# Repacking 64-bit tables in 26 pieces of 512 columns, with the low halves subtracted on VectorE and the raw weight loads behind the gathers

## The chip, the cores and the metric

One core of one Trainium2 chip runs the whole program. The metric is the device time of one execution in microseconds (us). Engines are named as in the profile: PE is TensorE's matrix multiply, PEld its weight load, DVE is VectorE, ACT is ScalarE, POOL is GpSimd, SP is SyncE, which here only issues DMAs.

## The reference

Three layers follow one another, on 2 batches of 768 tokens with 512 channels.

- Attention with 8 heads of 64: each token sees a local window of 96 tokens and 8 global ones, with a bias that falls with distance; then a softmax and the product with v.
- A mixture of 8 experts (512 to 1024 to 512, relu): each token goes to the expert with the largest logit, or to the one of the token before it, as a gate says; the result is weighted by the softmax of the logits.
- A mixing layer. With `theta = x @ w_theta` it is

```
zr, zi = x * cos(theta), x * sin(theta)
y = w_tok_r @ zr + w_tok_i @ zi          # over the 768 tokens of a batch
u = x + y
out = u + relu(u @ w_ch)
```

The three tables of the last layer, `w_theta` (512 x 512), `w_tok` (1536 x 768, r and i stacked) and `w_ch` (512 x 512), reach the chip as 64-bit floats. The kernel makes of each number a 32-bit float, and splits that into a high part (fp32r) and a low part, since its matmuls run in fp32r, three of them for one product.

## The kernel before, in words

**Attention** (lines 431 to 964). 24 steps of two units each; a unit is two heads of one block of 128 tokens. In a step PE makes the scores (`qk`, L542), DVE adds the bias and takes the maximum (`soft`, L564), ACT takes the exponential (L574), PE transposes (L597) and multiplies with v (L621). The routing of earlier blocks is put between (`route_stages`). A list, TAIL, orders what is left after step 23, with the work of a first group of 128 tokens ("lead") on PE. SP issues the loads of q, k, v.

**Experts** (lines 966 to 1601). The experts are taken by their number of tokens, ranks r = 0 to 7. Rows of x are gathered from DRAM by POOL's indirect DMA (`gather_x`, L1004) and transposed by PE (`x_tr`, L1288). The loop `for u in range(64)` takes a slice of 128 hidden units of rank r = u // 8: `mm1(u + 2)` (L1443, or L1427 for the small ranks), `mm2(u)` (L1480, L1490), `split_w1(u + 3)`, `split_w2(u + 1)`, `relu(u + 2)` (L1457, L1462). In ranks 0 to 3 w1 is split in two as well (ACT L1313, DVE L1314); w2 is split in all ranks (ACT L1410, then L1411 on POOL for ranks 0 to 3 but for u = 1, and on DVE for ranks 4 to 7). The raw weights come in 32 pieces of two 512 KB loads each, issued by SP in the order of the program (`load_piece`, L988 for w1, L992 for w2), with three buffers of each kind. SP reads the expert's number from `order_i` into a register before a load (L981). At u = 1 SP stores the weights of the tokens (`pd`, L1580); POOL gathers them back by slot (`gather_p`, L1354).

**Table jobs** (lines 354 to 418). A job repacks 256 columns of 128 rows: a load into `jraw`, ACT L391 (absolute value), DVE L392, L394, L396, L398 (put the 32 bits together, drop what is too small), ACT L401 (high part), and POOL L404 (low part). There are 52 jobs, w_theta first, then w_tok by rows, then w_ch. A job is a generator: `job_tick` runs it up to its next `yield`, so its steps are spread by hand over the program. After L401 a job issues the load of the job two further on. In the expert loop each u has 6 ticks and a job takes 10 of them (JLAG); in the last layer there are 18 places (JT), and `job_upto` forces what is due.

**Mixing layer** (lines 1604 to 1926). Twelve blocks k of 128 tokens. In the turn of block k PE does `h_mix(k, 0..3)` (48 matmuls of L1736), `h_theta(k + 2)` (L1660) and a transposition; DVE, ACT and POOL make sine and cosine of block k + 2 (`trig_*`, L1670 to L1716, of which L1692 and one L1716 are on POOL). `h_u` adds the sums of a batch, `h_out` makes the output (L1773).

Of the kernel before, what the change touches and what calls it, by code (L numbers as in the profile page):

```python
# [95 lines left out]
def kernel(  # L96
# [257 lines left out]
    jobs = []  # L354

    def add_jobs(src, dst, c, width):
        for o in range(0, width, 256):
            jobs.append((src[c * 128 : (c + 1) * 128, o : o + 256], dst, c, o))

    for c in range(4):  # L360
        add_jobs(w_theta, wth, c, DM)
    for t in range(NT):
        for c in (t, NT + t):
            add_jobs(w_tokT, None, c, S)
    for c in range(4):
        add_jobs(w_ch, wch, c, DM)

    def job_to(k):
        _, dst, c, o = jobs[k]
        return [(dst[i][:, c] if dst else wtok(i, c))[:, o : o + 256] for i in range(2)]  # L370
# [12 lines left out]
    def job(k):

        t = jraw.pop(k)
        lo, hi = t[:, :, 0], t[:, :, 1]
        w = jpool[0].tile([128, 256], I32, tag="jw", name="jw", bufs=2)
        m = jpool[0].tile([128, 256], F32, tag="jm", name="jm", bufs=2)
        wf = w.bitcast(F32)
        wh, wl = job_to(k)  # L390
        A.activation(m, hi.bitcast(F32), AF.Abs)  # L391
        V.tensor_scalar(w, hi, 3, 0x3FFFFFFF, op0=ALU.logical_shift_left, op1=ALU.bitwise_and)  # L392
        yield
        V.scalar_tensor_tensor(w, lo, 29, w, op0=ALU.logical_shift_right, op1=ALU.bitwise_or)  # L394
# [1209 lines left out]
    with ExitStack() as hctx:  # L1604
# [187 lines left out]
        ticks = {"n": 0, "done": 0, "per": nj / JT}

        def tick(n):
            ticks["n"] += n * ticks["per"]
            while ticks["done"] < ticks["n"]:
                job_tick()
                ticks["done"] += 1
# [192 lines left out]
```

## Time and profile before

| | |
|---|---|
| three runs | 525.34, 518.68, 524.3 us; median 524.3 us |
| the profiled execution | 524.86 us in all |
| its span, first to last instruction | 522.7 us |
| busy | PE 490.7, DVE 377.8, ACT 268.5, POOL 194.4 us |
| stages, us from the span's start | attention to 125, expert ranks 0 to 3 to 247, ranks 4 to 7 to 330, mixing layer to 522.7 |

The span leaves 2.2 us of the execution's own time around it. Busy time is an average over stages with different limits. A busy PE need not be a PE at its peak: the profile gives the clock that it was granted in a separate column (PEclk; 1.00 is 2.4 GHz, 0.50 is 1.2 GHz).

### The profile page before, as it was taken

What the parts mean: (1) busy time and instruction counts of PE and PEld (TensorE: products, weight loads), DVE (VectorE), ACT (ScalarE), POOL (GpSimd) and SP (SyncE); (2) the same over time, 40 slices, a digit from 0 to 9 for tenths busy, and PEclk for the clock granted to TensorE, in tenths of its full rate; (3) what the DMA queues carried; (4) which work ended last, traced back from release to release, by engine and by line L of the source; (5) the groups of instructions that cost most, each with busy time, mean ns of one, the idle gap of its engine ahead of it and who ended that gap; (6) DMA issues with size and microseconds to landing.
All of it is one profiled execution on the core that took longest, in us unless ns stands there. A gap on an engine that the chain in (4) does not pass through costs nothing.

```text
span 522.7 us, 9734 instructions
## 1 busy us (share of the span) xinstructions
PE 490.7 (94%) x3328; PEld 392.3 (75%) x3330; DVE 377.8 (72%) x1005; ACT 268.5 (51%) x686; POOL 194.4 (37%) x224
## 2 busy tenths in 40 slices
PE   9999999997979899899999999999998899999994
PEld 4676767686767788788777776788877688888884
DVE  6778787673957999789675868557888997672421
ACT  5886867513535756475545566445455444640200
POOL 3002223121656858476432325203444434360400
PEclk9999999998997999799999999999999989999999
DMA  8776759128557877666888986320122210001122
GB/s 242 244 204 205 234 183 324 46 73 276 145 131 250 271 222 252 216 227 198 283 278 270 289 281 226 97 81 20 25 76 82 80 42 20 22 0 50 33 95 72
DMA packets 65226, 83.20 MB, mean 159 GB/s; under 512 B 6816, under 2 KB 41248, under 8 KB 65168
## 3 DMA queue, kind: packets, MB, share of 16 engines
q1 hardware_dynamic: 54244, 61.18, 37.3%
q10 hardware_dynamic: 8156, 14.29, 8.3%
q0 software_dynamic: 2768, 7.02, 4.7%
q8 instruction: 28, 0.46, 0.4%
q14 instruction: 30, 0.25, 0.2%
HBM read 71.14 MB, written 11.34 MB: 158 GB/s over the span
## 4 chain that ended last, share of the span: by engine, by line
PE 55%; DVE 24%; DMA 7%; ACT 7%; issue 5%; ACTq 0%; POOL 0%; DVEq 0%
PE a L1736 10%; PE b L1773 6%; PE h L1427 6%; PE o L1480 6%; PE h L1443 4%; PE x L621 3%; DVE jw L396 3%; DVE jw L394 3%; PE s L542 3%; PE pt L597 3%; PE o L1490 3%; DMA jraw<-in_w_theta_dram 3%; DMA jraw<-in_w_tokT_dram 2%; DVE w1s L1314 2%; PE th L1660 2%
## 5 line engine op out<-in xcount | busy, mean ns | idle before, releaser
L1736 PE MATMUL a<-wtokr,z 128*128 128x512 f32 x480 | 86.1, 337 | 0.1
L1736 PEld LDWEIGHTS a<-wtokr,z 128*128 128x128 f32 x480 | 73.4, 188 | 10.0 <-POOL wtokr L404 0.4
L1480 PE MATMUL o<-w2s,hh 128*128 128x512 f32 x192 | 66.6, 426 | 3.3 <-POOL w2s L1411 2.9
L1443 PE MATMUL h<-xT,w1s 128*128 128x256 f32 (+1 forms) x384 | 60.0, 306 | 8.1 <-DVE w1s L1314 7.5
L1443 PEld LDWEIGHTS h<-xT,w1s 128*128 128x128 f32 x384 | 54.1, 204 | 13.4 <-DVE w1s L1314 10.2
L574 ACT ACTIVATE pr<-sm,st 128x256 f32<-128x256 f32 (+1 forms) x96 | 46.0, 481 | 19.2 <-DVE st L564 18.2
L1411 POOL TENSOR_TENSOR w2s<-raw,w2s 128x512 fp32r<-128x512 f32 x31 | 42.6, 1376 | 28.6 <-ACT w2s L1410 26.8
L404 POOL TENSOR_TENSOR wtokr<-jw,wtokr 128x256 fp32r<-128x256 f32 x30 | 24.1, 803 | 61.7 <-ACT wtokr L401 61.7
L1427 PE MATMUL h<-xT,raw 128*128 128x192 f32 (+1 forms) x256 | 46.0, 323 | 0.0
L564 DVE CUSTOM_DVE_ANT_0 sm<-s,bias 128x256 f32<-128x256 f32 (+1 forms) x96 | 34.0, 396 | 13.7 <-PE s L542 13.5
L1427 PEld LDWEIGHTS h<-xT,raw 128*128 128x128 f32 x256 | 38.5, 190 | 7.0 <-issue 6.6
L1410 ACT ACTIVATE w2s<-raw 128x512 fp32r<-128x512 f32 x64 | 39.7, 621 | 3.0 <-ACT yo L1526 2.7
L1480 PEld LDWEIGHTS o<-w2s,hh 128*128 128x128 f32 x192 | 34.0, 194 | 8.2 <-POOL w2s L1411 3.7
L394 DVE SCALAR_TENSOR_TENSOR jw<-jraw,jw 128x256 int32<-128x256 int32 x52 | 37.8, 727 | 1.6
L1480 PE MATMUL o<-w2s,hl 128*128 128x512 f32 x96 | 38.8, 405 | 0.0
L1457 ACT ACTIVATE hh<-h 128x256 fp32r<-128x256 f32 (+1 forms) x64 | 20.8, 324 | 30.9 <-PE h L1443 17.1
L396 DVE SCALAR_TENSOR_TENSOR jw<-jraw,jw 128x256 int32<-128x256 int32 x52 | 34.7, 667 | 0.9
L392 DVE TENSOR_SCALAR jw<-jraw 128x256 int32<-128x256 int32 x52 | 25.0, 480 | 12.5 <-DMA jraw<-in_w_theta_dram 6.8
L1314 DVE TENSOR_TENSOR w1s<-raw,w1s 128x512 fp32r<-128x512 f32 x32 | 29.6, 925 | 3.6 <-ACT w1s L1313 2.9
L391 ACT ACTIVATE jm<-jraw 128x256 f32<-128x256 f32 x52 | 22.2, 427 | 17.4 <-DMA jraw<-in_w_tokT_dram 8.9
L1411 DVE TENSOR_TENSOR w2s<-raw,w2s 128x512 fp32r<-128x512 f32 x33 | 23.2, 704 | 10.2 <-ACT w2s L1410 9.7
L398 DVE SCALAR_TENSOR_TENSOR jw<-jm,jw 128x256 f32<-128x256 f32 x52 | 26.7, 514 | 3.4 <-DVE jw L396 0.5
(266 smaller groups left out, 997.3 us busy)
## 6 DMA issues: line engine op xcount, KB each, us to landing
raw<-in_w_dram SPq DMA_DIRECT2D x64, 512.0 KB
jraw<-in_w_tokT_dram ACTq DMA_DIRECT2D x33, 256.0 KB
vv<-in_pack_dram SPq DMA_DIRECT2D x10, 512.0 KB
w<-in_w_dram SPq DMA_DIRECT2D x16, 256.0 KB
kall<-in_pack_dram SPq DMA_DIRECT2D x10, 320.0 KB
xd<-xt SPq DMA_DIRECT2D x12, 256.0 KB
q<-in_pack_dram SPq DMA_DIRECT2D x11, 256.0 KB
yd<-yo ACTq DMA_DIRECT2D x11, 256.0 KB
```

What stands on the lines that cost most here:

```text
L394: V.scalar_tensor_tensor(w, lo, 29, w, op0=ALU.logical_shift_right, op1=ALU.bitwise_or)
L396: V.scalar_tensor_tensor(w, hi, -1073741824, w, op0=ALU.bitwise_and, op1=ALU.bitwise_or)
L564: V.tensor_tensor_reduce(out=sm[:, hh, 0:W], in0=ust[u]["s"][hh], in1=bias[:, 2 * j + hh], scale=-0.125, scalar=BIG, op0=ALU.add, op1=ALU.min,
L574: A.activation(pr[:, hh, 0:W], sm[:, hh, 0:W], AF.Exp, bias=st[:, hh : hh + 1], scale=-1.0, accum_out=sums[n][:, 2 * j + hh : 2 * j + hh + 1],
L1314: (second or V).tensor_tensor(l1, s1, f32(h1), op=ALU.subtract)
L1410: A.activation(h2, bb[:, o], AF.Copy)
L1411: (V if RCAP[u // 8] <= FEW or u in W2V else G).tensor_tensor(l2, bb[:, o], f32(h2), op=ALU.subtract)
L1427: PE.matmul(hp[:, :N], lhsT=pieces[u // 2][1][:, j, o * 128 : (o + 1) * 128], rhs=x[:, j, :N], start=(j == 0), stop=(j == 3),)
L1443: PE.matmul(hp[:, :N], lhsT=wa[:, j], rhs=xa[:, j, :N], start=(k == 0), stop=(k == 11))
L1480: PE.matmul(out[:M], lhsT=ha[:, lo : lo + M], rhs=wa, start=(f == 0 and q == 0), stop=(f == 7 and q == 2),)
L1736: PE.matmul(acc[b][d][o], lhsT=za[:, d * 128 : (d + 1) * 128], rhs=wa[:, lo:hi], start=(t == 0 and n == 0 and (o == 0 or d % 2 == 0)), sto ...
L1773: PE.matmul(op[:, : hi - lo], lhsT=wa[:, d, e * 128 : (e + 1) * 128], rhs=ua[d][:, lo:hi], start=(n == 0), stop=(n == 11),)
```

## The change

- The tables are cut in 26 jobs of 512 columns; two ends of 256 columns of w_tok make one job with two loads. The first three jobs (the rows of w_tok for block 0) now run within attention, with their loads on SP's queue and the low part on POOL: one tick at the end of 15 of the steps, the rest ahead of TAIL.
- In the expert loop the ticks are metered: none in rank 0, 1.3 a slice in ranks 1 to 3, 2.4 in ranks 4 to 7 (up to u = 60). A job now takes 6 ticks. In the mixing layer there are 6 ticks a block.
- All low parts of w2, and from the experts on those of the jobs, are subtracted on DVE.
- The second raw load (w2 of piece 0) moves into the list LOADS, behind the first three gathers, and SP takes the experts' numbers from a copy that POOL makes after issuing those gathers.
- `pex` and `psum_` share memory with two tiles that are done.

```diff
-JT = 18
-JLAG = 5
-T0, T1, T2, T3 = 0, 2, 2, 14
+JATT = (4, 5, 6, 8, 9, 10, 12, 13, 14, 16, 17, 18, 20, 21, 22)
+JRATE = (0, 1.3, 1.3, 1.3, 2.4, 2.4, 2.4, 2.4)
+T1, T2, T3 = 2, 2, 2
...
-LOADS = ((1, 1), (1, 2), (2, 1), (2, 2))
+LOADS = ((1, 1), (0, 2), (1, 2), (2, 1), (2, 2))
...
+    def tok_ends(t):
+        def dst():
+            return [(wtokr[i][:, 2 * t - 2 : 2 * t] if t else wtok0[i])[:, :, 512:S] for i in range(2)]
+        return [w_tokT[c * 128 : (c + 1) * 128, 512:S] for c in (t, NT + t)], dst
+    tok_jobs = [[tok_piece(t, 0), tok_piece(t, 1), tok_ends(t)] for t in range(NT)]
+    jobs = tok_jobs[0] + [piece(w_theta, wth, c) for c in range(4)]
+    for t in range(1, NT):
+        jobs += tok_jobs[t]
+    jobs += [piece(w_ch, wch, c) for c in range(4)]
-    jstate = {"k": 0, "loaded": 0, "gen": None, "lag": JLAG, "bufs": 2, "eng": A}
+    jstate = {"k": 0, "loaded": 0, "gen": None, "bufs": 2, "eng": SP, "sub": G}
...
-            t = jpool[0].tile([128, 256, 2], I32, tag="jraw", name="jraw", bufs=jstate["bufs"])
+            t = jpool[0].tile([128, 512, 2], I32, tag="jraw", name="jraw", bufs=jstate["bufs"])
...
-        w = jpool[0].tile([128, 256], I32, tag="jw", name="jw", bufs=2)
-        m = jpool[0].tile([128, 256], F32, tag="jm", name="jm", bufs=2)
+        w = jtmp.tile([128, 512], I32, tag="jw", name="jw", bufs=1)
+        m = jtmp.tile([128, 512], F32, tag="jm", name="jm", bufs=1)
...
-        for _ in range(jstate["lag"]):
-            yield
+        yield
...
-        G.tensor_tensor(wl, wf, f32(wh), op=ALU.subtract)
+        jstate["sub"].tensor_tensor(wl, wf, f32(wh), op=ALU.subtract)
...
-            if s in (15, 16):
+            if s in (1, 2):
                 job_load()
+            if s in JATT:
+                job_tick()
...
+        job_upto(3)
...
-            regs[k] = SP.value_load(order_i[0:1, r : r + 1] if n else first_i, min_val=0, max_val=E - 1)
+            regs[k] = SP.value_load(order_g[0:1, r : r + 1] if n else first_i, min_val=0, max_val=E - 1)
...
-    load_piece(0)
+    load_piece(0, (1,))
     for n in range(1, 4):
         gather_x(n)
+    order_g = ct([1, 8], I32, "order_g")
+    G.tensor_copy(order_g, order_i)
...
-            (V if RCAP[u // 8] <= FEW or u in W2V else G).tensor_tensor(l2, bb[:, o], f32(h2), op=ALU.subtract)
+            V.tensor_tensor(l2, bb[:, o], f32(h2), op=ALU.subtract)
...
-        jstate["lag"] = JLAG
-        quick = [0]
+        jstate["eng"], jstate["sub"] = A, V
+        quick = [0.0]
...
-                if go:
-                    quick[0] += TF[min(r, 2) if r < 5 else 3]
+                if u < JL:
+                    quick[0] += JRATE[r] / 6
                     job_tick(int(quick[0]))
...
-                job_upto(8 + 6 * (k + 1))
+                job_upto(7 + 3 * k)
```

## Rows read from the trace of the kernel before

**Rows 1.** The page: PE's and the others' busy time; the chain by engine.
```profile
PE 490.7 (94%) x3328; PEld 392.3 (75%) x3330; DVE 377.8 (72%) x1005; ACT 268.5 (51%) x686; POOL 194.4 (37%) x224
...
PE 55%; DVE 24%; DMA 7%; ACT 7%; issue 5%; ACTq 0%; POOL 0%; DVEq 0%
```

**Rows 2.** Windows by stage: length, busy PE, PEld, DVE, ACT, POOL, clock, DMA share, GB/s.
```profile
18.30:91.30 73.00, 70.80 (x739) 51.54 (x736) 57.30 (x282) 57.25 (x189) 14.46 (x24) 1.00 0.74 225
...
125.00:164.70 39.70, 36.69 (x240) 29.57 (x240) 28.56 (x60) 16.66 (x39) 21.18 (x20) 0.87 0.63 177
164.70:247.50 82.80, 75.11 (x452) 65.56 (x449) 74.75 (x115) 51.26 (x114) 56.69 (x50) 0.96 0.72 230
247.50:330.00 82.50, 82.27 (x555) 59.00 (x555) 58.74 (x175) 44.98 (x111) 28.54 (x32) 1.00 0.80 261
...
353.40:388.10 34.70, 34.70 (x194) 29.94 (x193) 29.53 (x52) 18.14 (x38) 14.87 (x13) 1.00 0.12 33
388.10:431.30 43.20, 37.86 (x194) 31.15 (x193) 39.04 (x69) 20.30 (x44) 18.63 (x19) 0.96 0.24 73
```

**Rows 3.** Windows of tile jw alone: busy DVE, ACT, POOL, clock, DMA, GB/s.
```profile
125.00:164.70 39.70, 12.76 (x16) 1.64 (x4) 2.77 (x4) 0.87 0.63 177
164.70:247.50 82.80, 44.25 (x60) 6.22 (x15) 12.79 (x15) 0.96 0.72 230
247.50:330.00 82.50, 27.56 (x68) 7.01 (x17) 14.36 (x18) 1.00 0.80 261
353.40:445.00 91.60, 39.16 (x64) 6.67 (x16) 12.34 (x16) 0.98 0.17 49
```

**Rows 4.** Lines 394 and 392 by themselves: shortest, median and longest, ns.
```profile
L394 DVE SCALAR_TENSOR_TENSOR jw<-jraw,jw x52: 418/426/2852, 132.0 to 439.6; 128x256 int32<-128x256 int32 x52
...
L392 DVE TENSOR_SCALAR jw<-jraw x52: 277/291/1466, 131.0 to 438.1; 128x256 int32<-128x256 int32 x52
```

**Rows 5.** The timeline around 208 us: DVE and POOL.
```profile
207.44 2.18 DVE L396 SCALAR_TENSOR_TENSOR jw<-jraw,jw 128x256 int32<-128x256 int32 x1
...
208.05 1.27 POOL L1411 TENSOR_TENSOR w2s<-raw,w2s 128x512 fp32r<-128x512 f32 x1
```

**Rows 6.** The page's costliest groups: w2's low part on each of its engines.
```profile
L1411 POOL TENSOR_TENSOR w2s<-raw,w2s 128x512 fp32r<-128x512 f32 x31 | 42.6, 1376 | 28.6 <-ACT w2s L1410 26.8
...
L1411 DVE TENSOR_TENSOR w2s<-raw,w2s 128x512 fp32r<-128x512 f32 x33 | 23.2, 704 | 10.2 <-ACT w2s L1410 9.7
```

**Rows 7.** Groups by shape: w1's low part (164.7 to 247.5 us); L1676 at 512 columns.
```profile
L1314 DVE TENSOR_TENSOR w1s<-raw,w1s 128x512 fp32r<-128x512 f32 x22 | 22.3, 1014 | 2.7 <-ACT w1s L1313 2.3
...
L1676 DVE SCALAR_TENSOR_TENSOR rr<-kk,rr 128x512 f32<-128x512 f32 x10 | 6.9, 692 | 0.3
```

**Rows 8.** Waits of the whole span: us in total, times, longest.
```profile
DVE sm L564 <- PE s L542: 13.5, 16, 1.5
...
PE h L1443 <- DVE w1s L1314: 7.5, 7, 2.8
...
DVE jw L392 <- DMA jraw<-in_w_tokT_dram: 5.0, 5, 2.0
...
PE tr L1288 <- DMA xg<-xd,xidx: 2.9, 2, 1.8
```

**Rows 9.** The timeline from 153 to 159 us: POOL and DVE behind DMAs.
```profile
153.11 0.96 POOL L1354 DMA_INDIRECT ps<-pd,xidx  x1 [4.76 <-DMA pd<-ptok]
...
158.65 0.29 DVE L392 TENSOR_SCALAR jw<-jraw 128x256 int32<-128x256 int32 x1 [6.83 <-DMA jraw<-in_w_theta_dram]
```

**Rows 10.** Windows of one matmul line alone, L1443 and then L1736: busy PE, PEld.
```profile
222.55:227.95 5.40, 3.03 (x24) 2.96 (x24) 1.00 0.58 183
...
353.45:388.10 34.65, 25.66 (x146) 21.92 (x145) 1.00 0.12 32
388.20:431.20 43.00, 27.46 (x145) 22.34 (x144) 0.96 0.24 73
```

**Rows 11.** The chain of waits: a 256 KB load of jraw, issue to landing.
```profile
303.73 6.73 DMA jraw<-in_w_tokT_dram
```

More of the change, by code (lines that the diff above doesn't have):

```diff
@@ L47 @@
 TWO_PI = 6.283185307179586
-NJ1 = 52
 NWARM = 14
@@ L71 @@
 JL = 61
-TF = (1, 1, 1, 1)
 W0, W1 = 8, 0
-LOADS = ((1, 1), (1, 2), (2, 1), (2, 2))
+LOADS = ((1, 1), (0, 2), (1, 2), (2, 1), (2, 2))
 PU = 1
@@ L78 @@
 GP = 4
-W2V = (1,)
 HU = 36
-JF = 0
 XL = 0
@@ L352, in wtok, with piece, tok_piece @@
         return wtokr[i][:, 2 * t - 2 + n] if t else wtok0[i][:, n]
[L354 to L370, printed above, removed]
-    jstate = {"k": 0, "loaded": 0, "gen": None, "lag": JLAG, "bufs": 2, "eng": A}
+    def piece(src, dst, c):
+        return [src[c * 128 : (c + 1) * 128, 0:512]], lambda: [x[:, c] for x in dst]
+    def tok_piece(t, n):
+        c = n * NT + t
+        return [w_tokT[c * 128 : (c + 1) * 128, 0:512]], lambda: [wtok(i, c)[:, 0:512] for i in range(2)]
+    def tok_ends(t):
[8 more added lines that the diff above has]
+    jstate = {"k": 0, "loaded": 0, "gen": None, "bufs": 2, "eng": SP, "sub": G}
     jraw = {}
@@ L377, in job_load @@
         if k < len(jobs):
-            t = jpool[0].tile([128, 256, 2], I32, tag="jraw", name="jraw", bufs=jstate["bufs"])
-            jstate["eng"].dma_start(t, jobs[k][0].bitcast(I32).rearrange("p (c w) -> p c w", w=2))
+            t = jpool[0].tile([128, 512, 2], I32, tag="jraw", name="jraw", bufs=jstate["bufs"])
+            W = 512 // len(jobs[k][0])
+            for i, src in enumerate(jobs[k][0]):
+                jstate["eng"].dma_start(
+                    t[:, i * W : i * W + W], src.bitcast(I32).rearrange("p (c w) -> p c w", w=2)
+                )
             jraw[k] = t
@@ L386, in job @@
         lo, hi = t[:, :, 0], t[:, :, 1]
-        w = jpool[0].tile([128, 256], I32, tag="jw", name="jw", bufs=2)
-        m = jpool[0].tile([128, 256], F32, tag="jm", name="jm", bufs=2)
+        w = jtmp.tile([128, 512], I32, tag="jw", name="jw", bufs=1)
+        m = jtmp.tile([128, 512], F32, tag="jm", name="jm", bufs=1)
         wf = w.bitcast(F32)
-        wh, wl = job_to(k)
+        wh, wl = jobs[k][1]()
         A.activation(m, hi.bitcast(F32), AF.Abs)
@@ L398, in job @@
         V.scalar_tensor_tensor(wf, m, MIN64, wf, op0=ALU.is_ge, op1=ALU.mult)
-        for _ in range(jstate["lag"]):
-            yield
+        yield
+        wf = wf.rearrange("p (i c) -> p i c", c=wh.shape[-1]) if len(wh.shape) == 3 else wf
         A.activation(wh, wf, AF.Copy)
@@ L427 @@
     jctx = ExitStack()
-    jpool = [jctx.enter_context(tc.tile_pool(name="jb", bufs=1, reuse_waits="tile"))]
+    jtmp = jctx.enter_context(tc.tile_pool(name="jb", bufs=1, reuse_waits="tile"))
+    jpool = [jtmp]
     with ExitStack() as actx:
@@ L1018 @@
     slot0 = ct([128, 1], F32, "slot0")
-    pex = ct([128, NB, 8], F32, "pex")
-    psum_ = ct([128, NB], F32, "psum_")
+    pex = posall
+    psum_ = mxall
     def probs():
@@ L1550 @@
         relu(1)
-        jstate["lag"] = JLAG
-        quick = [0]
+        jstate["eng"], jstate["sub"] = A, V
+        quick = [0.0]
         for u in range(64):
             r, f = divmod(u, 8)
-            go = jstate["k"] * 64 <= u * NJ1 and JF <= u < JL
             def tick():
-                if go:
-                    quick[0] += TF[min(r, 2) if r < 5 else 3]
+                if u < JL:
+                    quick[0] += JRATE[r] / 6
                     job_tick(int(quick[0]))
@@ L1787 @@
         us[1] = [[wtok(i, c) for c in (0, NT, 1, NT + 1)] for i in range(2)]
-        nj = len(jobs) - jstate["k"]
-        jstate["lag"] = 1
         jstate["bufs"] = JBUFS
         jpool[0] = jctx.enter_context(tc.tile_pool(name="jb2", bufs=1, reuse_waits="tile"))
[L1792 to L1798, printed above, removed]
         for k in range(1, 4):
@@ L1897 @@
                 h_u(b, 1)
-            trig_a(k + 2, tick=lambda: tick(T0))
+            trig_a(k + 2)
             h_xh(k + 3)
@@ L1901 @@
             h_xl(k + 3)
-            tick(T1)
+            job_tick(T1)
             if k == HS:
@@ L1909 @@
             trig_b(k + 2)
-            tick(T2)
+            job_tick(T2)
             h_mix(k, 3)
@@ L1914 @@
             trig_c(k + 2)
-            tick(T3)
+            job_tick(T3)
             if k == HS:
```

## The prediction

> **What bounds the kernel now.** I read the page first, for who is busy: PE 490.7 of 522.7 us, and DVE next with 377.8; the chain that ended last lies 55% on PE and 24% on DVE [rows 1]. So PE sets the time and DVE interrupts it somewhere. The windows by stage say where [rows 2]. Attention (18.3 to 91.3) has PE at 70.8 of 73.0 us. Ranks 4 to 7 (247.5 to 330) have it at 82.27 of 82.5, at the full clock. The loss is in three other stretches: rank 0 (125 to 164.7) with 3.0 us of idle PE and a granted clock of 0.87; ranks 1 to 3 (164.7 to 247.5) with 7.7 us idle, a clock of 0.96 and DVE busy 74.75 of 82.8; and blocks k = 4 to 6 of the mixing layer (388.1 to 431.3) with 5.3 us idle, a clock of 0.96 and DVE 39.04 of 43.2.
>
> What DVE spends its time on there is read from tile jw alone [rows 3]. A job has four DVE instructions. Unhindered they take 0.291 + 3 x 0.426 = 1.57 us, by the medians [rows 4]. In ranks 4 to 7 they do: 27.56 us for 17 jobs, 1.62 each. In ranks 1 to 3 a job costs 44.25 / 15 = 2.95 us, in the mixing layer 39.16 / 16 = 2.45. The longest L394 took 2.85 us [rows 4]. The difference between the stages is POOL: where jobs are slow, POOL does 512-wide subtractions beside them. The timeline shows a case, a 0.42 us DVE step that lasts 2.18 us while a subtraction of 1.27 us runs on POOL [rows 5]. L1314 suffers as well: 1.014 us on average in ranks 1 to 3 [rows 7] against 0.704 for the same shape where POOL has no w2 work [rows 6], and PE waits 7.5 us for it [rows 8].
>
> The Trainium skill has a rule for it ("SBUF — State Buffer", section "Who interferes with whom"): a VectorE instruction with two SBUF inputs, or in a two-port mode, and a GpSimd instruction that reads SBUF shut each other out for their whole length, whichever began first. The trace agrees in kind (2.18 us above). By that rule all of the stretch in ranks 1 to 3 goes, and the term below for them would be -11 in place of -8, 504 us in all; but the two POOL steps a block that stay in the mixing layer (L1692, L1716) would go on holding DVE, which speaks for its -7 and not -8.4.
>
> **The change part by part.** The sum is made against the profiled execution, 524.9 us (522.7 of span and 2.2 around it); the median of the runs shown is 524.3.
>
> *Prices.* A 512-wide step with two inputs is 0.692 us [rows 7]. The one-input step, half as dear per column, I put at 0.291 + 0.133 = 0.42 (0.133 is half of 0.692 - 0.426); it lies between 0.29 and 0.58. So a wide job is 0.42 + 3 x 0.692 = 2.50 us on DVE, plus 0.70 for its subtraction [rows 6], 3.20 in all. It replaces two old jobs of 1.57 (unhindered) to 2.95. Per w2 slice DVE takes on 0.70, and POOL loses 1.376 [rows 6].
>
> *Attention, three jobs in 15 ticks.* New on DVE: 3 x 2.50 = 7.5 us; on ACT two steps a job, each at most twice the 0.41 of L401 (6.22 us for 15, [rows 3]), 5 us in all; on POOL three subtractions. The cover is DVE's wait for PE's scores, 13.5 us in 16 places [rows 8], and 73.0 - 57.3 = 15.7 us of idle DVE [rows 2]. The steps are at the end of a turn, where that wait is. The ends are 0 and 7.5 (all of DVE's part shows); I take +1.5, near the lower end, since the cover is twice the cost. The two early loads (512 KB each) go into SP's queue ahead of the loads of the fourth block, which is used only two blocks on; no cost, at most 2 us (0.5 MB at 225 GB/s, [rows 2]).
>
> *Gathers first.* PE waits 2.9 us for the gathered rows [rows 8], with the raw loads on the DMA engines beside them. Behind the gathers come the copy and the register load, then w1 of piece 1 and w2 of piece 0; behind the waiting SP instruction are only raw loads. The first of these is used only by the third `mm1` and the first `mm2`. The ends are -3 and +2 (w2 of piece 0 late for `mm2(0)`); I take -2.5.
>
> *Rank 0.* The change takes away two blocked queues [rows 9]. DVE waited 6.83 us for a job's load; rank 0 has no jobs now. POOL waited 4.76 us for the `pd` store, with w2's subtractions queued behind; they are on DVE now. What stays: that store still holds up the raw loads behind it on SP's queue. To win back are 3.0 us of idle PE and the lost clock: 0.13 x 39.7 = 5.2 us, together 8.2 [rows 2]. I take -5; the ends are 0 and -8.
>
> *Ranks 1 to 3.* DVE: 74.75 less 44.25 of jobs, less 22 x (1.014 - 0.70) = 7 us of stretch, plus 24 x 1.3 / 6 = 5.2 wide jobs x 3.20 = 16.6, plus 24 x 0.70 = 17: some 57 of 75 us, so DVE stops being the bound. PE's own pace is 5.4 us for two slices [rows 10], so 24 slices take 65 us, plus transpositions; idle and lost clock (0.04 x 82.8 = 3.3) say the same, 82.8 - 7.7 - 3.3 = 72. I take -8 of 11, as each slice still goes PE, ACT, DVE, PE with DVE at three quarters.
>
> *Ranks 4 to 7.* 29 slices x 2.4 / 6 = 11.6 wide jobs, worth 23 old ones, for 17 before. DVE: 58.74 - 27.56 + 11.6 x 3.20 = 68 of 82.5 us. Loads: 261 GB/s x 82.5 = 21.5 MB, plus 11.6 x 0.52 - 17 x 0.26 = 1.6 MB, so 280 GB/s; at the 0.80 share that carried 261 that is a share of 0.86. Hidden behind PE, but for one thing: DVE and ACT stand in order behind jraw (5.0 us of DVE's waits are that, [rows 8]), and a 256 KB load took 6.73 us [rows 11]. A load now has 7 ticks, 2.9 slices, 7.5 us before its use, and twice the bytes. I take +3; the ends are 0 and +23 (below).
>
> *Mixing layer.* 3 + 16.8 jobs are done before it, so 6.2 remain, 6.2 x 3.20 = 20 us of DVE for 39.16. Blocks 1 to 3 took 34.65 us, blocks 4 to 6 took 43.0 for the same matmuls [rows 10], so 8.4 is the gain if DVE stops stretching PE. I take -7; the ends are 0 and -8.4.
>
> Sum: +1.5 - 2.5 - 5 - 8 + 3 - 7 = -18, so 507 us.
>
> **The rivals.** *The gain stays in the experts' first half.* Attention shows all 7.5, and the wait for jraw eats 8 in ranks 4 to 7: 6 + 5 more than the forecast, 518 us. For it: DVE is at 57.3 of 73.0 in attention, and its queue is in order. Against: the idle places are where the ticks go.
>
> *Late loads of jraw (slower).* A load has 7.5 us until its use. If the second 256 KB come at half the rate that the core reaches in this stage (130 GB/s, 2 us more), a load lands after 8.7 us, 1.2 us late, about what the lead of a slice hides. If instead they take another 6.73 us [rows 11], it lands after 13.5 us. Two loads are under way at a time, so the job between waits too and lengthens the lead: DVE and ACT stand still (13.5 - 7.5) / 2 = 3 us a job, less one that is hidden, 11.6 x 2 = 23 us, and 507 - 3 + 23 = 527. It decides from a landing of about 13 us up: then the rest of the gain is gone. Against: the waits before were at most 2.0 us each, and slices that wait also load more slowly, which frees the engines.
>
> The page of the Trainium skill named above (table under "A bandwidth-pool intuition that's wrong") puts HBM to one core at about 358 GB/s; by that the 280 GB/s have room and this rival falls away. No run here shows that figure.
>
> *DVE's stretch is not POOL's doing.* Then DVE in ranks 1 to 3 has the 57 us plus 7 on L1314 and, at two old jobs for one, 5.2 x (5.9 - 2.5) = 18; some 82 of 82.8 us, so nothing is won there, and 1 us in the mixing layer: 524.9 + 1.5 - 2.5 - 5 + 3 - 1 = 521 us. Against: the same instructions take 1.62 us beside a POOL without w2 work [rows 3].
>
> *All cover holds:* 0 - 3 - 8 - 11 + 0 - 8.4 = -30, 495 us.
>
> **How the numbers follow.** Forecast (500 to 514) 0.68; better than that, towards 495, 0.10; the gain only in the first half, or the stretch kept (515 to 522), 0.16; late loads (525 and over) 0.06. The range of 8 in 10 goes from 498 to 519. A measurement of this kernel tells about 2% from no change, 10.5 us: faster by more (under 513.8 us) 0.78, within 2% 0.16, slower by more 0.06.
>
> **What would show it.** Right: L394 and L1314 at one duration, near 0.69, through ranks 1 to 3; no POOL arithmetic from 120 to 330 us; the first L1443 some 2.5 us earlier against the end of the lead's matmuls; a clock of 1.00 from 165 to 240; blocks k = 4 to 6 of the mixing layer at about 11.6 us each. Wrong: waits of ACT L391 or DVE L392 for jraw of more than 15 us in ranks 4 to 7; PE's score matmuls waiting for DVE in attention; PE idle in ranks 1 to 3 behind DVE at 90% or more; raw loads that arrive late behind the copy of the experts' numbers.

## The result and the profile after

| | before | after |
|---|---|---|
| median (lowest to highest), us | 524.6 (518.68 to 525.34), 4 runs | 497.18 (495.95 to 498.89), 4 runs |
| the profiled execution; its span, us | 524.86; 522.7 | 495.95; 494.1 |

The ratio is 0.950, with a 95% interval of 0.943 to 0.958: faster by 27.4 us, where 18 were forecast. The median lies 0.8 us below the range's lower end.

The page of after, busy time and chain by engine, answers to [rows 1].

```profile
PE 478.5 (97%) x3328; PEld 385.0 (78%) x3330; DVE 353.8 (72%) x955; ACT 260.8 (53%) x634; POOL 117.4 (24%) x145
...
PE 79%; DVE 7%; DMA 6%; ACT 4%; issue 2%; ACTq 0%; SPq 0%; DVEq 0%; POOLq 0%
```

PE's share of the span goes from 94 to 97%, and its share of the chain from 55 to 79%; DVE's falls from 24 to 7%. DVE is as busy as before, at 72% of the span, but little of the chain that ended last is its own now.

The windows of after by stage (columns as in [rows 2]): attention, rank 0, ranks 1 to 3, ranks 4 to 7, blocks 1 to 3 and blocks 4 to 6 of the mixing layer.

```profile
18.30:92.10 73.80, 70.43 (x731) 50.99 (x728) 62.41 (x291) 58.98 (x193) 16.94 (x26) 1.00 0.77 240
122.80:156.30 33.50, 32.71 (x241) 26.06 (x241) 21.91 (x56) 15.65 (x33) 9.07 (x9) 1.00 0.78 226
156.30:226.90 70.60, 70.18 (x453) 62.92 (x450) 53.15 (x100) 45.13 (x92) 12.35 (x12) 1.00 0.79 259
226.90:308.90 82.00, 81.82 (x554) 58.83 (x552) 65.81 (x165) 45.45 (x100) 13.24 (x13) 1.00 0.83 275
332.40:367.30 34.90, 34.90 (x194) 29.93 (x193) 30.96 (x47) 20.83 (x40) 14.20 (x10) 1.00 0.12 39
367.30:402.40 35.10, 35.10 (x194) 30.00 (x193) 30.50 (x47) 15.53 (x28) 11.05 (x9) 1.00 0.13 39
```

Against [rows 2], ranks 1 to 3 take 70.6 us for 82.8, with PE busy in 70.18 of them; rank 0 33.5 for 39.7; blocks 4 to 6 35.1 for 43.2, PE without a gap. Ranks 4 to 7 are as long as before. With the starts of the stages taken from the same matmul of each kernel, the two spans differ by these terms:

| stage | forecast | measured |
|---|---|---|
| attention and the tail behind it | +1.5 | +0.3 (76.8 to 78.2, then 29.8 to 28.7) |
| from the gathered rows to the first `mm1` | -2.5 | -2.0 |
| rank 0 | -5 | -6.2 |
| ranks 1 to 3 | -8 | -12.2 |
| ranks 4 to 7 | +3 | -0.3 |
| blocks 4 to 6 | -7 | -8.1 |
| all else | 0 | -0.2 |

DVE's operations by shape in ranks 1 to 3 of after answer to [rows 4, 6, 7]; the columns are busy us, mean ns, idle time before.

```profile
L1422 DVE TENSOR_TENSOR w2s<-raw,w2s 128x512 fp32r<-128x512 f32 x24 | 16.5, 686 | 0.8 <-ACT w2s L1421 0.8
L1325 DVE TENSOR_TENSOR w1s<-raw,w1s 128x512 fp32r<-128x512 f32 x20 | 13.8, 688 | 7.5 <-ACT w1s L1324 7.4
L1473 DVE SCALAR_TENSOR_TENSOR hl<-h,hh 128x256 fp32r<-128x256 f32 x22 | 9.3, 421 | 4.4 <-ACT hh L1468 4.4
L400 DVE SCALAR_TENSOR_TENSOR jw<-jraw,jw 128x512 int32<-128x512 int32 x5 | 3.4, 684 | 0.0
L398 DVE SCALAR_TENSOR_TENSOR jw<-jraw,jw 128x512 int32<-128x512 int32 x5 | 3.4, 684 | 0.0
L396 DVE TENSOR_SCALAR jw<-jraw 128x512 int32<-128x512 int32 x6 | 2.5, 420 | 0.0
```

L1325, the subtraction of w1, was L1314 of before: 1014 ns there, 688 here. All the wide two-input steps shown have the one duration, 684 to 688 ns; POOL has no arithmetic in this stretch.

Tile jw alone in ranks 1 to 3 and 4 to 7 (length, busy DVE, ACT, POOL, clock, DMA share, GB/s) answers to [rows 3].

```profile
156.30:226.90 70.60, 16.20 (x26) 3.14 (x5) 0.00 (x0) 1.00 0.79 259
226.90:308.90 82.00, 36.98 (x58) 6.93 (x11) 0.00 (x0) 1.00 0.83 275
```

A job has five DVE steps now, so 58 of them are 11.6 jobs, and 36.98 / 11.6 = 3.19 us a job; the forecast had 11.6 jobs of 3.20.

The loads of the tables in after (KB each, median us from issue to landing) answer to [rows 11].

```profile
jraw<-in_w_tokT_dram ACTq DMA_DIRECT2D x10, 512.0 KB, 4.7
...
jraw<-in_w_tokT_dram ACTq DMA_DIRECT2D x10, 256.0 KB, 5.0
```

Twice the bytes land in 4.7 us, less than the 6.73 of the one load in [rows 11]. The 4.7 is the median of the four loads of 512 KB whose landing the trace has: 3.7, 4.2, 5.1 and 7.5 us. Neither ACT nor DVE has a wait for jraw among after's waits, and PE's 7.5 us for w1's low part [rows 8] have become 0.6:

```profile
PE h L1454 <- DVE w1s L1325: 0.6, 2, 0.4
```

### The profile page after: what moved, and what is told of

The parts are those of the page before. It is cut to its first block, busy times and chain, and to the rows that moved or that the text cites. A ratio compares the mean times of both kernels' runs of the same rounds, so it can differ in the third digit from the quotient of the medians.

```text
span 494.1 us, 9501 instructions
## 1 busy us (share of the span) xinstructions
PE 478.5 (97%) x3328; PEld 385.0 (78%) x3330; DVE 353.8 (72%) x955; ACT 260.8 (53%) x634; POOL 117.4 (24%) x145
## 3 DMA queue, kind: packets, MB, share of 16 engines
q1 hardware_dynamic: 53812, 61.97, 39.4%
## 4 chain that ended last, share of the span: by engine, by line
PE 79%; DVE 7%; DMA 6%; ACT 4%; issue 2%; ACTq 0%; SPq 0%; DVEq 0%; POOLq 0%
PE a L1746 21%; PE o L1491 11%; PE h L1454 8%; PE b L1783 7%; PE th L1670 6%; PE h L1438 6%; PE s L547 3%; PE x L626 3%; PE o L1501 3%; PE pt L602 2%; DVE sm L569 2%; DMA yd<-yo 2%; DMA jraw<-in_w_tokT_dram 2%; PE h L757 2%; PE y L768 2%
## 5 line engine op out<-in xcount | busy, mean ns | idle before, releaser
L1422 DVE TENSOR_TENSOR w2s<-raw,w2s 128x512 fp32r<-128x512 f32 x64 | 44.0, 688 | 14.7 <-ACT w2s L1421 14.6
L1454 PE MATMUL h<-xT,w1s 128*128 128x256 f32 (+1 forms) x384 | 53.4, 288 | 1.2 <-DVE w1s L1325 0.6
L569 DVE CUSTOM_DVE_ANT_0 sm<-s,bias 128x256 f32<-128x256 f32 (+1 forms) x96 | 34.0, 395 | 10.3 <-PE s L547 10.1
L1012 POOL DMA_INDIRECT xg<-xd,xidx x17 | 16.8, 986 | 85.0 <-PE tr L1299 78.6
L602 PE MATMUL pt<-ident,pr 128*128 128x128 f32 x176 | 26.0, 280 | 4.5 <-DVE xt L652 3.2
L1325 DVE TENSOR_TENSOR w1s<-raw,w1s 128x512 fp32r<-128x512 f32 x32 | 22.1, 690 | 9.6 <-ACT w1s L1324 9.4
L1791 DVE SCALAR_TENSOR_TENSOR ob<-b,xTf 128x512 f32<-128x512 f32 (+1 forms) x16 | 8.8, 556 | 27.6 <-PE b L1783 27.5
L1702 POOL TENSOR_TENSOR si<-si,yg 128x512 f32<-128x512 f32 x10 | 13.4, 1343 | 60.0 <-ACT si L1695 50.8
L1473 DVE SCALAR_TENSOR_TENSOR hl<-h,hh 128x256 fp32r<-128x256 f32 (+1 forms) x64 | 22.4, 350 | 6.0 <-ACT hh L1468 6.0
L602 PEld LDWEIGHTS pt<-ident,pr 128*128 128x128 f32 x176 | 19.2, 141 | 9.4 <-DVE xt L652 3.8
L547 PE MATMUL s<-kall,q 64*128 64x256 f32 (+1 forms) x192 | 25.6, 385 | 0.0
```

What stands on the lines that cost most here:

```text
L547: PE.matmul(sp[hh][:, 0:W], lhsT=qs[n][half, j], rhs=kall[half, b, j, t * 160 + 160 - W : t * 160 + 160], start=True, stop=True,)
L569: V.tensor_tensor_reduce(out=sm[:, hh, 0:W], in0=ust[u]["s"][hh], in1=bias[:, 2 * j + hh], scale=-0.125, scalar=BIG, op0=ALU.add, op1=ALU.min,
L602: PE.transpose(pt[:, hh, c], pr[:, hh, c * 128 : (c + 1) * 128], ident)
L1422: V.tensor_tensor(l2, bb[:, o], f32(h2), op=ALU.subtract)
L1454: PE.matmul(hp[:, :N], lhsT=wa[:, j], rhs=xa[:, j, :N], start=(k == 0), stop=(k == 11))
```

## The experiments

Twelve runs follow. Theory A: POOL work that reads SBUF holds DVE's steps, and the change wins by taking it away from beside the jobs in ranks 1 to 3. Its rivals: the 512-wide steps themselves win, or the metering (no jobs in rank 0), or the places of the jobs. Each expectation names the one that it is set against. "Before" of each set was run on the same chip: 521.6, 521.3 and 522.4 us.

### Only w2's subtractions moved, in the kernel before

```diff
-            (V if RCAP[u // 8] <= FEW or u in W2V else G).tensor_tensor(l2, bb[:, o], f32(h2), op=ALU.subtract)
+            V.tensor_tensor(l2, bb[:, o], f32(h2), op=ALU.subtract)
```

> The kernel before with one part of the change alone: all low parts of w2 on DVE; jobs, ticks and loads as before. Theory A (POOL's reads stretch DVE): DVE takes on 24 x 0.69 = 17 us in ranks 1 to 3 and loses some 20 to 25 of stretch, so 67 to 72 of the stage, PE nearly free: ranks 1 to 3 from 82.8 to 74-78 us, rank 0 4 us shorter (POOL's queue is out of the way), 508 to 514 us against some 522 to 524. Theory B (only the smaller number of jobs helps): DVE has 75 + 17 = 92 us of work in a stage of 83, so 5 to 10 us slower than before, 527 to 534 us.

Measured: 510.56 us, ratio 0.978 (0.972 to 0.985), as theory A had it, though ranks 1 to 3 fell below its 74 to 78 us and rank 0 lost 2.2 us where 4 were expected. The window of ranks 1 to 3, first all work, then tile jw alone (columns as in [rows 2, 3]):

```profile
162.50:235.20 72.70, 71.67 (x451) 62.93 (x449) 62.47 (x134) 48.55 (x110) 25.57 (x27) 1.00 0.80 259
```

```profile
162.50:235.20 72.70, 23.70 (x58) 6.18 (x15) 12.96 (x15) 1.00 0.80 259
```

One line changed, and DVE's busy time in the stretch falls from 74.75 to 62.47 us although it has 24 subtractions more: 15 jobs take 23.70 us, 1.58 each, where they took 2.95 [rows 3]. The stretch takes 72.7 us instead of 82.8. That is most of the change's gain in this stage, with narrow jobs, the old metering and the old order of gathers. Nor was it that PE waited for POOL's own result, 1.4 us long where DVE's takes 0.7: all of PE's waits in this stage of before are the 7.5 us for DVE's L1314 [rows 8]. Blocks 4 to 6 keep 42.8 us.

### The same subtractions put back, in the kernel after

```diff
-            V.tensor_tensor(l2, bb[:, o], f32(h2), op=ALU.subtract)
+            (V if RCAP[u // 8] <= FEW or u == 1 else G).tensor_tensor(l2, bb[:, o], f32(h2), op=ALU.subtract)
```

> The changed kernel with one part undone: the low parts of w2 of ranks 0 to 3 are subtracted on POOL again, as before. The changed kernel takes 497.2 us; by stage rank 0 33.5, ranks 1 to 3 70.6, ranks 4 to 7 82.0 us. Theory A (POOL's reads of SBUF stretch DVE, and DVE then stops PE): L1314's counterpart goes from 0.69 to about 1.0 us again, rank 0 +3 to +5 (POOL's queue behind the pd gather too), ranks 1 to 3 +4 to +8, 503 to 509 us in all. Theory B (the gain is that fewer jobs are done in ranks 0 to 3; where a subtraction runs matters little): rank 0 +3 for POOL's queue alone, ranks 1 to 3 0 to +1, about 500 us.

Measured: 503.83 us, 0.962 (0.956 to 0.968). The profiled execution is the longest of the four, 506.71 us where the others took 498.70 to 504.08, so its stages are rather too long for the median. It has rank 0 at 39.0 us (33.5 in after) and ranks 1 to 3 at 74.4 (70.6). Windows of both:

```profile
123.60:162.60 39.00, 35.61 (x240) 28.13 (x240) 19.46 (x46) 15.85 (x33) 19.86 (x17) 0.91 0.76 197
162.60:237.00 74.40, 71.11 (x452) 63.08 (x449) 60.04 (x79) 44.96 (x92) 46.08 (x37) 1.00 0.74 242
```

DVE's groups in the second:

```profile
L1325 DVE TENSOR_TENSOR w1s<-raw,w1s 128x512 fp32r<-128x512 f32 x21 | 22.5, 1072 | 6.2 <-ACT w1s L1324 6.1
...
L400 DVE SCALAR_TENSOR_TENSOR jw<-jraw,jw 128x512 int32<-128x512 int32 x5 | 7.8, 1565 | 0.0
...
L396 DVE TENSOR_SCALAR jw<-jraw 128x512 int32<-128x512 int32 x6 | 3.6, 599 | 0.0
```

The steps are held again (L1325 1072 ns for 688, L400 1565 for 684), and so is one of the six of L396, which has one input in SBUF: it takes 1505 ns and lifts the mean to 599 from 420. But only 3.8 us come back in ranks 1 to 3, where 10.1 went in the experiment above: with the metered wide jobs DVE is busy 60.04 of 74.4 us, hold and all, and bears most of it. In rank 0 PE idles 3.4 us and the granted clock falls to 0.91. Of its waits there 2.2 us are for ACT's high part of w2, with ACT itself waiting 5.6 us for raw loads (2.4 in after), and 1.1 us for POOL.

### Useless POOL work put beside DVE

The edit adds to each slice of ranks 0 to 3 (but u = 1) a subtraction on POOL into memory that is written again later; nobody needs it.

```diff
             V.tensor_tensor(l2, bb[:, o], f32(h2), op=ALU.subtract)
+            if u < 32 and u != 1:
+                G.tensor_tensor(wch[1][:, 0], y0, f32(h2), op=ALU.subtract)
```

> The changed kernel with work added that nobody waits for: after each w2 subtraction on DVE in ranks 0 to 3, POOL subtracts tiles of the same shape (128x512, two SBUF inputs, one of them the fresh high part) into an unused tile. It adds 31 steps of 1.3 us on POOL and takes none off DVE. Theory A: DVE's steps with two SBUF inputs stretch again, L1314's counterpart to 0.9 us or more, DVE busy in ranks 1 to 3 up from 53 by 12 to 25 us, and the stage 3 to 10 us longer: 501 to 508 us. Theory B: no change, 497 us, with DVE at 53 us.

Measured: 505.89 us, 0.967 (0.962 to 0.972), 8.7 us over after. The profiled execution, 509.26 us, is the longest of the four. Ranks 1 to 3 take 80.6 us for 70.6; every other stage is within 0.7 us of after, but for 1.2 us ahead of attention. The window of ranks 1 to 3 (columns as in [rows 2]), DVE's groups in it, and a stretch of the timeline (start, duration):

```profile
156.20:236.80 80.60, 75.02 (x457) 62.60 (x456) 75.33 (x96) 44.90 (x93) 51.84 (x37) 1.00 0.73 235
```

```profile
L1422 DVE TENSOR_TENSOR w2s<-raw,w2s 128x512 fp32r<-128x512 f32 x23 | 26.1, 1134 | 1.8 <-ACT w2s L1421 1.8
L1325 DVE TENSOR_TENSOR w1s<-raw,w1s 128x512 fp32r<-128x512 f32 x22 | 19.3, 876 | 4.2 <-ACT w1s L1324 4.2
L1475 DVE SCALAR_TENSOR_TENSOR hl<-h,hh 128x256 fp32r<-128x256 f32 x23 | 9.5, 412 | 0.0
L398 DVE SCALAR_TENSOR_TENSOR jw<-jraw,jw 128x512 int32<-128x512 int32 x5 | 7.1, 1430 | 0.0
```

```profile
171.28 1.30 POOL L1424 TENSOR_TENSOR wch<-y,w2s 128x512 fp32r<-128x512 f32 x1 [0.21 <-ACT w2s L1421]
...
171.71 1.43 DVE L402 SCALAR_TENSOR_TENSOR jw<-jm,jw 128x512 f32<-128x512 f32 x1
...
173.79 1.56 PE L1456 MATMUL h<-xT,w1s 128*128 128x256 f32 x11 [0.57 <-DVE w1s L1325]
...
175.47 3.28 POOL L1424 TENSOR_TENSOR wch<-y,w2s 128x512 fp32r<-128x512 f32 x2 [0.90 <-ACT w2s L1421]
...
175.79 1.79 DVE L1422 TENSOR_TENSOR w2s<-raw,w2s 128x512 fp32r<-128x512 f32 x1
```

L402 begins 0.43 us after POOL's subtraction and lasts 1.43 us, 0.56 us beyond the subtraction's end; L1325 behind it is late, and PE waits 0.57 us for it (brackets). At 175.79 the same befalls L1422. All 24 DVE steps of the stage that last over 0.9 us end 0.55 to 0.56 us after a subtraction of POOL's; after has no such step there. L1475 has one input in PSUM and keeps its 412 ns. PE's waits in the stage are 4.7 us for w1's low part, 0.5 for w2's and 0.3 for L1475, all on DVE; no engine waits for the subtractions on POOL. So the hold by itself costs 10 us in this execution (8.7 in the median), and this run shows the mechanism alone: 5.5 us are PE's waits, and the rest is a PE that is shown as busy for 75.02 us in place of 70.18, at the full clock.

### The kernel after once more

No edit; it ran in the second set, beside three of the kernels here.

> The changed kernel on this chip, for comparison with the other runs of this call: 494 to 499 us, stages as in its first profile within 1.5 us each (rank 0 33.5, ranks 1 to 3 70.6, ranks 4 to 7 82.0).

Measured: 497.12 us, 0.953 (0.947 to 0.959), the first result again. Against the 521.3 us of before on this chip that is 24.1 us; of the 27.4 above, some 3 us are before's, whose median was 524.6 there.

### Job steps cut in halves, in the kernel after

```diff
-        V.tensor_scalar(w, hi, 3, 0x3FFFFFFF, op0=ALU.logical_shift_left, op1=ALU.bitwise_and)
+        for c in halves:
+            V.tensor_scalar(w[:, c], hi[:, c], 3, 0x3FFFFFFF, op0=ALU.logical_shift_left, op1=ALU.bitwise_and)
```

The other DVE steps of a job likewise.

> The changed kernel with every DVE step of a job issued as two halves of 256 columns, loads and ticks unchanged. A job then costs DVE 2 x (0.29 + 4 x 0.425) = 4.0 us in place of 3.2, 21 us more in all. Theory A (DVE is no longer the bound): 497 to 499 us, DVE's busy time up by some 20 us. Theory C (the width of the steps is the gain, since it takes the fixed part off DVE): 503 us or more.

Measured: 499.58 us, 0.956 (0.953 to 0.960), between the two theories' ranges. Ranks 1 to 3 take 70.9 us, so the width does nothing there; the profiled execution is 2.4 us longer in ranks 4 to 7. The 21 us more on DVE did not come either: it is busy 360.1 us for 353.8, as the second half of a step begins 0.33 us after the first, which lasts 0.42. In this kernel, where DVE has room, 2 to 3 us are the width's; whether it would be worth more in the kernel before was not run.

### The jobs' own subtractions back on POOL, in the kernel after

```diff
-        jstate["eng"], jstate["sub"] = A, V
+        jstate["eng"], jstate["sub"] = A, G
```

> The changed kernel with one part undone: the low parts of the jobs run on POOL in the expert loop and the mixing layer as well (23 jobs, one 1.3 us step each). Theory A: 23 steps can stretch 23 to 46 DVE steps by up to 1.3 us, spread over stages where DVE has 20% room: 497 to 501 us, most of it in the mixing layer. Theory B: 497 us. A third theory, that POOL's latency at the end of a job was what held the tables back: over 503 us.

Measured: 498.07 us, 0.955 (0.951 to 0.958): no difference from after that can be told. Ranks 1 to 3 take 70.8 us and blocks 4 to 6 35.1. One held step a job is borne; the 24 of w2 in ranks 1 to 3 were not.

### All subtractions of w2 and the jobs moved, in the kernel before

The edit of the first experiment, and in L404:

```diff
-        G.tensor_tensor(wl, wf, f32(wh), op=ALU.subtract)
+        V.tensor_tensor(wl, wf, f32(wh), op=ALU.subtract)
```

> The kernel before with w2's subtractions and the jobs' own all on DVE; 52 narrow jobs, metering and gathers as before. Theory A (a job's place decides in the mixing layer): ranks 1 to 3 as with w2 alone on DVE (72 to 74 us against 82.8), blocks 4 to 6 still 39 to 44 us, the whole 507 to 512. Rival (its subtractions on POOL made the mixing layer long): blocks 4 to 6 come down to 35 to 37 us and the whole to 500 to 505.

Measured: 512.33 us, 0.981 (0.978 to 0.985), 0.3 us above theory A's range. Ranks 1 to 3 take 71.3 us, so no more than 0.7 us of this stage is left to wide jobs, metering and gathers; blocks 4 to 6 take 44.9. So POOL's subtractions of the jobs are not what made these blocks long, and the rival of that falls.

### No jobs in rank 0, in the kernel before

```diff
-JF = 0
+JF = 8
```

> The kernel before with no job ticks in rank 0 (nothing else). The jobs left out there, 4 of the old size, are done later, in the end in the mixing layer. Theory: DVE's 6.8 us wait for a load behind the pd store goes, but POOL's queue still waits for that store with w2's low parts behind it: rank 0 from 39.7 to 35-37 us. The mixing layer's blocks 4 to 6 get 4 x 2.45 = 10 us more of DVE work and are 5 to 10 us longer. In all 520 to 530 us, so the metering alone is no gain. Rival (metering is the gain): 515 us or less.

Measured: 534.66 us, 1.025 (1.018 to 1.032): slower than before, and by more than was expected. Rank 0 falls to 34.5 us (39.7 before), but the jobs that it shed come due in the mixing layer. Its window of blocks 4 to 6, and PE's waits there:

```profile
385.70:437.50 51.80, 41.75 (x193) 34.08 (x192) 44.06 (x80) 21.38 (x48) 20.76 (x21) 0.87 0.24 77
```

```profile
PE th L1660 <- DVE rr L1674: 3.5, 1, 3.5
PE a L1736 <- DVE xTf L1748: 3.3, 1, 3.3
PE a L1736 <- ACT wtokr L401: 3.3, 2, 1.7
```

These blocks take 51.8 us for 43.2 and blocks 1 to 3 39.3 for 34.7. A rank 0 without jobs is worth 5 us only to a kernel that has another place for them.

### No jobs in attention, in the kernel after

```diff
-JATT = (4, 5, 6, 8, 9, 10, 12, 13, 14, 16, 17, 18, 20, 21, 22)
+JATT = ()
...
-        job_upto(3)
```

> The changed kernel without its three jobs in attention, so that all 26 are left for the experts and the mixing layer. Theory A (the mixing layer is shorter because fewer jobs are left in it): attention goes back from 78.2 to 76.8 us, some 9 jobs in place of 6 stay for the mixing layer, 3 x 3.2 us more for a DVE that was busy 30.5 of 35.1 us in blocks 4 to 6, so those blocks take 40 to 44 us again and the whole 501 to 506. Rival (the mixing layer is shorter because its subtractions left POOL): blocks 4 to 6 stay under 37 us and the whole is 495 to 498.

Measured: 505.31 us, 0.970 (0.965 to 0.975), 8 us over after. Attention goes back to 76.8 us, blocks 4 to 6 take 44.5. PE's waits in those blocks:

```profile
PE a L1745 <- ACT wtokr L405: 6.7, 2, 3.6
```

The windows of blocks 4, 5 and 6 (columns as in [rows 2]):

```profile
367.30:382.30 15.00, 11.99 (x66) 10.01 (x64) 13.81 (x19) 7.63 (x15) 7.32 (x5) 1.00 0.19 59
382.30:400.10 17.80, 14.12 (x63) 11.70 (x64) 8.51 (x15) 3.21 (x7) 0.00 (x0) 0.81 0.19 69
400.10:411.80 11.70, 11.70 (x66) 9.99 (x64) 11.42 (x19) 5.87 (x12) 3.63 (x3) 1.00 0.23 69
```

Tile jw from 370 to 415 us and from 415 to 500:

```profile
370.00:415.00 45.00, 16.65 (x21) 2.52 (x4) 0.92 0.20 65
415.00:500.00 85.00, 11.34 (x13) 1.90 (x3) 1.00 0.12 42
```

The size is as expected, the reason only in part. Three more jobs stand in the mixing layer, but DVE is not the bound: its last jobs come after these blocks (13 steps from 415 us on; after has none there), and PE waits 6.7 us for rows of `w_tok` that are needed and not split yet, after which its clock is granted at 0.81 from 382.3 to 400.1 us. In the kernel before, PE waited there for DVE's own work of the blocks (2.7 us for `xTf`, 2.5 us for `rr`) and PEld for ACT (3.1 us for `xTf`, 2.8 us for a table). After has neither kind of wait. That fewer jobs left for these blocks is what took both away is shown for the tables, by this run, and argued for DVE's own work. Three early jobs, at +1.4 us in attention, buy 8 in all.

### The order of the gathers alone, in the kernel before

```diff
-LOADS = ((1, 1), (1, 2), (2, 1), (2, 2))
+LOADS = ((1, 1), (0, 2), (1, 2), (2, 1), (2, 2))
...
-    load_piece(0)
+    load_piece(0, (1,))
...
+    order_g = ct([1, 8], I32, "order_g")
+    G.tensor_copy(order_g, order_i)
```

> The kernel before with the order of loads alone: w2 of piece 0 behind the gathers, the experts' numbers from POOL's copy. Theory: first matmul of the experts 2 to 2.5 us after the first transposition in place of 4.0, and all of it kept at the end unless a stage behind eats it: 520 to 523 us, not to be told from before by time, but in the trace. Rival: the raw loads come late and mm2(0) waits, 525 us.

Measured: 518.65 us, 0.994 (0.991 to 0.996): 3 us or so, small but real. The stretch to the first `mm1` takes 2.0 us in place of 4.0. The windows of rank 0 and of ranks 1 to 3 (columns as in [rows 2]):

```profile
121.30:160.70 39.40, 33.34 (x241) 26.14 (x241) 27.85 (x60) 16.75 (x39) 21.98 (x20) 1.00 0.87 225
160.70:240.60 79.90, 72.40 (x449) 63.06 (x450) 74.91 (x115) 51.27 (x114) 57.29 (x51) 1.00 0.74 239
```

The clock is granted in full in both, where before had 0.87 and 0.96. Ranks 1 to 3 are 2.9 us shorter, with DVE as busy as before. Rank 0 is not: it takes 39.4 us for 39.7, with 6.1 us of idle PE for 3.0.

### Attention's three subtractions on DVE, in the kernel after

```diff
-    jstate = {"k": 0, "loaded": 0, "gen": None, "bufs": 2, "eng": SP, "sub": G}
+    jstate = {"k": 0, "loaded": 0, "gen": None, "bufs": 2, "eng": SP, "sub": V}
```

> The changed kernel with the subtractions of attention's three jobs on DVE in place of POOL. Theory A (POOL's reads hold DVE, and in attention that shows as the one turn that takes 1 us longer): attention 77.0 to 77.7 us in place of 78.2, the whole 495.5 to 497. Rival (DVE's 3 x 0.69 us more is dearer there than POOL's hold): 78.5 us or more, the whole 497.5 to 499.

Measured: 498.71 us, 0.956 (0.952 to 0.959); attention 78.1 us. The turn that took 5.7 us takes 5.2, and another goes from 4.8 to 5.2. What one turn gains another gives back: the time lies where the rival had it, attention where neither had it, and this is no better version.

### Rows of 2 KB for the jobs' loads, in the kernel after

```diff
-        return [src[c * 128 : (c + 1) * 128, 0:512]], lambda: [x[:, c] for x in dst]
+        return [src[c * 128 : (c + 1) * 128, o : o + 256] for o in (0, 256)], lambda: [x[:, c] for x in dst]
```

> The changed kernel with each job's load of 512 columns as two transfers of 256 (rows of 2 KB in place of 4 KB), the same bytes. If the length of a row made the loads land early: landing 6 to 8 us in place of 4.7, DVE and ACT wait for jraw in ranks 4 to 7 for 3 to 10 us, the whole 498 to 505. If the load of the queues did, and not the row: 4 to 6 us, no such wait, 496.5 to 498.

Measured: 500.29 us, 0.956 (0.951 to 0.960). The loads on ACT's queue:

```profile
jraw<-in_w_tokT_dram ACTq DMA_DIRECT2D x30, 256.0 KB, 4.8
```

They land in 4.8 us, and neither ACT nor DVE waits for jraw: the length of a row is not what made them early. The time lies where the other theory had it, 3 us above after's; the profiled execution has 2.7 of them in rank 0 and 2.8 in ranks 4 to 7, and the runs don't say why; that execution, 502.22 us, is the longest of its four. The intervals of the two ratios overlap.

## Why the prediction was right, and where it was too small

**Ranks 1 to 3: the cause right, the term too small (-8 forecast, -12.2 measured).** The step "less 44.25 of jobs" held: jobs fell to 16.20 us where 16.6 were forecast, DVE to 53.15 where 57 were. Two steps below it were off. "-8 of 11, as each slice still goes PE, ACT, DVE, PE with DVE at three quarters" took 3 us off for a chain that costs nothing: PE idles 0.42 us. And the end of 11 itself was too near: it took idle PE (7.7) and the lost clock (3.3), but a PE that is shown as busy was also slowed. The same matmuls kept PE busy 75.11 us in before [rows 2] and 70.18 in after, 4.9 less, of which the clock explains 3.3 by the prediction's working. The rest shows at the full clock as well: 72.40 us in the kernel before with its gathers moved, 75.02 with useless POOL work. What lengthens a busy PE there the profile doesn't tell.

Behind this stands the rule of the Trainium skill ("SBUF — State Buffer", section "Who interferes with whom") that the prediction weighed against its own value. By it all of the stretch was to go, 504 us in all. The runs bear the rule out: with useless POOL work L398 and L408 took 1430 and 1435 ns for 684 and 686, and L1475, with an input in PSUM, did not change. One part of it, that the one that began first goes first, [rows 5] do not show: L396 has its start 0.61 us ahead of POOL's subtraction, needs 0.42 us, and still ends 0.30 us after it. The sum by the rule was nearer than mine. Its other use, that the two POOL steps a block left in the mixing layer "would go on holding DVE", came true for DVE and not for PE. DVE's and POOL's groups in blocks 4 to 6 of after:

```profile
L398 DVE SCALAR_TENSOR_TENSOR jw<-jraw,jw 128x512 int32<-128x512 int32 x3 | 5.0, 1670 | 0.1
```

```profile
L1726 POOL TENSOR_TENSOR z<-si,z 128x512 fp32r<-128x512 f32 x3 | 4.8, 1601 | 3.0 <-ACT z L1721 3.0
...
L1702 POOL TENSOR_TENSOR si<-si,yg 128x512 f32<-128x512 f32 x2 | 2.7, 1342 | 14.3 <-PE a L1746 9.2 <-ACT si L1695 5.1
```

L398 lasts 1670 ns beside them, yet DVE has 4.6 us to spare in 35.1, and PE no gap.

**Ranks 4 to 7 (+3 forecast, -0.3 measured).** The loads were feared late: "twice the bytes", a landing of 8.7 to 13.5 us against a lead of 7.5. They land in 4.7 in the median, and the latest of the four that are known in 7.5, the lead itself. The row of 6.73 us [rows 11] was a single load, taken from the chain that ended last; no row told where it stood among the others. The traces of three kernels with narrow jobs have the landings of some such loads: 4.0, 4.3 and 4.4 us in the median (no jobs in rank 0, gathers moved, all subtractions moved). The second of them:

```profile
jraw<-in_w_tokT_dram ACTq DMA_DIRECT2D x33, 256.0 KB, 4.3
```

So twice the bytes added 0.3 to 0.7 us, where the term feared 2.0 to 6.7. The rest of the working held: DVE 65.81 us (68 forecast), 275 GB/s (280), a DMA share of 0.83 (0.86). The rival of late loads is refuted as to landing; that halves of the same bytes gave 2.8 us more in this stage is left open.

**Mixing layer (-7, measured -8.1).** The size was right, the reason half, and so the size in part luck. The working had DVE's time for jobs fall to 20 us and the stretch with it. The jobs left were as forecast, 31 steps at five a job, so 6.2 jobs, but they are held, at 5.0 us each for 3.20 (tile jw, columns as in [rows 3]):

```profile
332.40:415.00 82.60, 31.11 (x31) 4.41 (x7) 0.00 (x0) 1.00 0.12 36
```

DVE's time for them fell from 39.16 [rows 3] to 31.11 us only. Moving the jobs' subtractions gave nothing (44.9 us in the kernel before, no loss in the kernel after). What gave it is when the jobs are done: without attention's three, tables miss their block.

**Rank 0 (-5, measured -6.2).** Two blocked queues were named, and the size is near. The bound of 8.2 us was not sound: it added the lost clock to the idle PE, and with the clock granted in full (gathers moved) the stage is as long as before, the time being spent as waiting. Which queue it was is not settled. PE waits for POOL in before's rank 0:

```profile
PE o L1480 <- POOL w2s L1411: 2.9, 1, 2.9
```

Without jobs in this rank that wait is 0.8 us. As to the time, in the kernel before, leaving the jobs out of this rank saved 5.2 us with w2 still on POOL, and w2 on DVE saved 2.2 with the jobs still there; but in the kernel after, without jobs, w2 back on POOL cost 5.5, in the longest execution of its four, with a part of it in late raw loads.

**Gathers (-2.5, measured -2.0), attention (+1.5, measured +1.4, and -1.1 in the tail).** As forecast; the tail's 1.1 us was not, but it takes 27.8 to 30.1 us in the changed kernel and its variants, so that is no difference that can be told.

**The rivals.** "The gain stays in the experts' first half" fell: attention shows 1.4 us of DVE's 7.5. "DVE's stretch is not POOL's doing" fell by three runs. "All cover holds" (495 us, given one chance in ten) is where the time went: the cautions at ranks 1 to 3, ranks 4 to 7, rank 0 and the mixing layer all erred to one side, by 4.2, 3.3, 1.2 and 1.1 us.

## What to carry to other kernels

When an instruction has a median far below its mean, look at what runs on the other engine in its longest cases, and price the move by the median: here one subtraction moved from POOL to DVE, the busier of the two, made DVE less busy by 12 us. Work that repacks tables for a later stage must be placed by when that stage needs it: emptying one stage of it cost 13 us where nothing else had room, and three early jobs bought 8 us for 1.4. The one load that the chain showed here was a late one, 6.73 us where such loads take 4.0 to 4.4 in the median: a single row may set an end of a range, but not a term of the sum.

## What was not expected of the hardware

A DVE operation of one element a partition can be held for a whole POOL subtraction. The timeline of after in attention:

```profile
41.26 1.26 POOL L408 TENSOR_TENSOR wtok<-jw,wtok 128x512 fp32r<-128x512 f32 x1
41.27 1.26 DVE L179 TENSOR_TENSOR gA<-gA,gt 128x1 f32<-128x1 f32 x1
...
42.57 0.16 DVE L180 TENSOR_TENSOR gA<-gA,gt 128x1 f32<-128x1 f32 x1
```

L179 has 128 x 1 elements and lasts 1.26 us, the length of POOL's L408 beside it; L180 of the same shape takes 0.16. With L408 on DVE, L179 takes 0.16 too.

A job's load of 512 KB, or of two halves of 256 KB, lands in 4.7 to 4.8 us in the median at a DMA share of 0.81 to 0.83, hardly later than the 4.0 to 4.4 us of single loads of 256 KB.
